# A fused attention and two-layer kernel: first output products inside the attention's plan, with new start and new places

## The chip, the cores and the metric

The kernel runs on one core of one Trainium2 chip. Times are device microseconds (us) from launch to end. An execution's profile gives its span, from the first to the last instruction, and the clock that TensorE was granted: 1.00 is its upper level of 2.4 GHz, 0.50 its lower of 1.2 GHz.

## The reference

```python
# q, k, v: (4, 8, 576, 64); tau a scalar
scores = scale * q @ k^T
thresh = max(scores) - tau
scores = where(scores >= thresh, scores, -1e9)
attn   = softmax(scores)              # sum + 1e-9
x      = attn @ v                     # as 2304 tokens x 512

# first layer, d_ff 1536
xn  = x / sqrt(mean(x * x) + 1e-6) * rms_g
g   = xn @ w_gate
x   = (silu(g) * (xn @ w_val)) @ w_out

# second layer, d_ff 2048
h   = x @ w2_in
out = (h * cos(h)) @ w2_out
```

The weights arrive in a wide number format; the kernel converts them on the chip. Products that need more than one pass are made from a high and a low half of each operand, three matmuls each (`mm3`).

## The kernel before

**Attention.** Heads are taken in 16 pairs, each cut into five units of up to 128 queries (`NU` = 80 units). For a pair, `load_k`, `load_q` and `load_v` issue its loads on SP's queue; `prep_pe` transposes keys ("b", "c") and queries ("a") on TensorE, and `prep_act` copies them out of PSUM on ScalarE. For a unit, `s_mm` makes scores in two PSUM tiles, `s_max` on VectorE moves them to SBUF with a running extreme, `s_exp` on ScalarE makes exponentials, `s_thr` on GpSimd the thresholds, and `s_mask` on VectorE the masked exponentials with their sums. `t_pe` and `c_pe` transpose these on TensorE, `t_raw` and `c_raw` copy them out, `av` multiplies by v into the one bank of the tag "v", and `av_out` copies the result. The sums are inverted (`r_inv`), written out (`r_out`) and read back over all partitions (`r_in`); `av_div` on GpSimd multiplies by them. Then `x_sq`, `x_add` (GpSimd) and `x_sum` (TensorE, into `pss`) make the mean square of each token, which is needed at the end of each batch of four pairs.

**The plan.** The order of the attention is not written by hand. `Plan.add` takes steps with an engine, a cost and a place from the table `STEPS`, and `Plan.order` simulates the engines. It repeatedly issues the step that can start first; `place`, which is the table's third number plus `at * UNIT`, decides between steps that can start at the same time. A TensorE step that changes the array's tiling (`TILING`: scores and `av`) can start only `SWITCH` (100 ns) later. Steps in `LOCK` keep VectorE and GpSimd apart in the simulation; those of `BEHIND` are also made to wait for the VectorE step ahead of them. `take` and `free` model the buffers: "t" has three PSUM banks, "v" one, "e" six. The engines then run their instructions in the issued order, each when its inputs are there.

At the start stand eight `warm` matmuls, two more behind the first transposes, and three after each of the first six units. While the attention runs, six weight jobs (`weight_job`, group 0 of the first layer) convert weights: a load, two integer steps on VectorE, one on ScalarE, one sum on GpSimd, then a high half on ScalarE and a low half by a subtraction on VectorE. The plan holds too the first chunk of the layer's input (`chunk(0, ...)`: `x_load`, `x_p`, `x_a`, `x_d`), chunks 1 and 2, and the first four gate and value products (`gv_mm` for n = 0 to 3, `N_EARLY`, each in two halves of 12 matmuls) with `h_silu`, `h_mul`, `h_hi` and `h_lo`.

**First layer.** Tokens go in six chunks of 384 and inner features in six groups of two tiles; `seq` lists (group, chunk, feature tile) as n = 0 to 71. Behind the plan a loop runs from n = 4: if `o1` is behind by more than one, an `o1` is run first; then come `gv_mm(n)` and `gv_h(n)`, and then the next `o1`. `o1(n)` multiplies with the output weights into four PSUM banks (`px`: three of "t" and the one of "v"); after the two tiles of a group it moves the four banks into `acc` on VectorE, by a copy in group 0 and by an addition later. `pump` advances the weight jobs between these steps. The second layer follows and is not touched.

Of the kernel before, what the change touches and what calls it, by code (L numbers as in the profile page):

```python
# [9 lines left out]
F32 = mybir.dt.float32  # L10
# [8 lines left out]
P = 128  # L19
# [6 lines left out]

UNIT = 3500
STEPS = {
    "none": ("", 0, 27559),
    "load_k": ("SP", 1700, -172962, 5000),  # L30
    "load_q": ("SP", 1700, -46102, 7000),
    "load_v": ("SP", 1700, -4761, 5000),
    "pb": ("PE", 440, -19143),
    "pa": ("PE", 440, -15661),
    "pc": ("PE", 330, -8379),
    "pb_a": ("ACT", 590, 81106),
    "pa_a": ("ACT", 690, -473960),
    "pc_a": ("ACT", 480, 49428),
    "s": ("PE", 960, -21325),
    "s4": ("PE", 490, 85459),  # L40
    "warm": ("PE", 640, 37404),
    "max": ("DVE", 833, -172383),
    "exp": ("ACT", 785, 72251),
    "th": ("POOL", 300, -18608),
    "mask": ("DVE", 890, -37373),
    "t": ("PE", 438, 31564),
    "raw": ("ACT", 595, -92045),
    "c0": ("PE", 220, -3639),
    "c1": ("PE", 440, -315186),
    "c_raw": ("ACT", 415, 218185),  # L50
    "radd": ("POOL", 250, 94231),
    "rinv": ("DVE", 430, -4519),
    "r_out": ("SP", 2100, -108544, 2500),
    "r_in": ("SP", 1700, -320774, 11000),
    "av0": ("PE", 2110, -371909),
    "av1": ("PE", 2660, -60188),
    "avo": ("ACT", 420, 4517),
    "div": ("POOL", 1410, 8372),
    "xout": ("SP", 500, -179658, 2500),
    "sq": ("POOL", 1145, 63241),  # L60
    "x_add": ("POOL", 1410, 86580),
    "xsum": ("PE", 1150, 399585),
    "mean": ("DVE", 150, -681609),
    "rms": ("POOL", 1520, 138440),
    "rs_out": ("SP", 2500, -32428, 2500),
    "x_load": ("SP", 500, 48239, 6000),
    "x_p": ("POOL", 1010, 169405),
    "x_a": ("ACT", 610, -116593),
    "x_d": ("DVE", 550, 94630),
    "jdma": ("SP", 500, 52341, 5000),  # L70
    "j1": ("DVE", 600, -115045),
    "j2": ("DVE", 690, -98093),
    "j_p": ("POOL", 1310, 466908),
    "j_a": ("ACT", 620, 67088),
    "gv": ("PE", 2100, 18969),
    "silu": ("ACT", 500, -124840),
    "hmul": ("DVE", 560, -259566),
    "hhi": ("ACT", 520, -319947),
    "hlo": ("DVE", 560, -244125),
}  # L80
SIGNAL = 100
SWITCH = 100

LOCK = {
    "mask", "j1", "j2", "x_d", "hlo", "th", "div", "sq", "x_add", "rms", "radd", "x_p", "j_p",
}
BEHIND = {"div", "sq", "x_add", "x_p", "j_p"}
# [9 lines left out]
N_EARLY = 4  # L97


class Plan:  # L100
# [19 lines left out]
    def order(self):  # L120
# [69 lines left out]
    def run(self, tc):  # L190


        done = tc.nc.cur_bb.bb.instructions
        wait = mybir.DependencyInfo(mybir.DependencyClass.Sync, mybir.DependencyReason.DATA)
        for s in self.order():
            n = len(done)
            s["fn"]()
            if s["eng"] == "DVE" and s["kind"] in LOCK:
                s["ins"] = done[-1]
            if s.get("behind"):  # L200
                for x in done[n:]:
                    tc.add_manual_dep(x, s["behind"]["ins"].name, wait, reason="port")


@with_exitstack
def attention_moe_cos_kernel(
# [81 lines left out]
    def weight_job(n, key, pool, stage, src, idle):  # L288
# [499 lines left out]
    def scale_x(c):  # L788
        nc.gpsimd.tensor_tensor(
            acc[c], acc[c], xrs[c][:, None, :].broadcast_to([P, KD, TC]), op=ALU.mult  # L790
        )

    def attention():

        plan = Plan({
# [23 lines left out]
        for p in range(NPAIRS):  # L819
            n = 5 * p  # L820
            if p:
                lk[p] = add("load_k", n, load_k, p, take=[("kn", ("kn", p))])
# [125 lines left out]
        for i, job in enumerate(jobs):  # L948
# [14 lines left out]
            jops.append(add("j2", at, step, after=[x], free=[("jtmp", i)] + ([] if wide else [("jraw", i)]),  # L963
            ))
        jobs.clear()

# [6 lines left out]
        def grow_2():  # L973
            att_s.close()
            late[2] = ctx.enter_context(tc.tile_pool(name="xhl2", bufs=1, side="right"))
            late["acc", 3] = ctx.enter_context(tc.tile_pool(name="acc3", bufs=1, side="right"))
            late["rs", 3] = ss_p

        ends = [mk[n, hd] for n in range(NU - 10, NU) for hd in heads(n)]
# [22 lines left out]
        for n in range(N_EARLY):  # L1002
# [6 lines left out]
            x = add("hmul", NU + n, h_mul, n, after=[x, y], free=[("gv", n)])  # L1009
            x = add("hhi", NU + n, h_hi, n, after=[x])  # L1010
            hs.append(add("hlo", NU + n, h_lo, n, after=[x], free=[("hh", n)]))
        plan.run(tc)

    with tc.manual_schedule():
        jobs += [
# [10 lines left out]
        acc_p = ctx.enter_context(tc.tile_pool(name="acc", bufs=NCH - 1))  # L1026
# [3 lines left out]
        late.update({("acc", c): acc_p for c in range(NCH) if c != 3})  # L1030
# [9 lines left out]
        xacc = {}  # L1040

        def o1(n):
            g, c, i = seq[n]
            fs = groups[g][1]
            if i == fs[0]:
                xacc[c] = [
                    (ps_t if d else ps_v).tile(
                        [P, 512], F32, tag="t" if d else "v", name=f"px{d}"
                    )[:, 0:TC]
                    for d in range(KD)  # L1050
                ]
            whi, wlo = slots["1", 2, i]
            h = hq.pop(n)
            for d in range(KD):
                mm3(xacc[c][d], (whi[:, d], wlo[:, d]), h, i == fs[0], i == fs[-1])
            if i == fs[-1]:
                if c not in acc:
                    acc[c] = acc_tile(c, [P, KD, TC])
                for d in range(KD):
                    dst = acc[c][:, d]  # L1060
                    if g == 0:
                        nc.vector.tensor_copy(dst, xacc[c][d])  # L1062
                    else:
                        nc.vector.tensor_tensor(dst, dst, xacc[c][d], op=ALU.add)
                del xacc[c]

        def split_x(c):
            for kk in range(KD):
# [191 lines left out]
```

## Time and profile before

| What | Value |
|---|---|
| Median of three runs | 1190.27 us (1190.05 to 1190.27) |
| Profiled execution, time | 1190.16 us |
| Its span | 1188.4 us |
| TensorE busy, of the span | 1162.2 us, 98% |
| VectorE busy | 798.9 us, 67% |
| ScalarE busy | 647.4 us, 54% |
| GpSimd busy | 313.8 us, 26% |
| Mean granted clock | 0.994 |

Engines are named PE (TensorE matmuls), PEld (its weight loads), DVE (VectorE), ACT (ScalarE), POOL (GpSimd) and SP (the queue that issues most loads). L524 is line 524 of the kernel. In a row "x<-y" reads as what is written and from what. A matmul's end is modelled, so consecutive rows can overlap a little; a matmul of two fp32 operands shows as two instructions. Idle time is given with the engine and line that ended it.

### The profile page before, as it was taken

The numbers are of one execution on the slowest core, as the hardware profiler recorded it, in microseconds if no ns is written. First come the engines' busy times: TensorE is split into PE (matmuls) and PEld (weight loads), VectorE is DVE, ScalarE is ACT, GpSimd is POOL, SyncE is SP. The second block draws the span as 40 slices with busy tenths as digits, with TensorE's granted clock in tenths as the row PEclk, the third lists the DMA queues.
The fourth block names the chain that finished last, engine by engine and source line by source line (L and its number), as shares of the span: only waits on it lengthen the run. The fifth ranks groups of instructions, "written<-read, shape, count | busy, mean of one in ns | idle before, by whom it ended". The sixth has DMA issues, their size and how long they took to land.

```text
span 1188.4 us, 18206 instructions
## 1 busy us (share of the span) xinstructions
PE 1162.2 (98%) x6832; PEld 1021.9 (86%) x6832; DVE 798.9 (67%) x1571; ACT 647.4 (54%) x1210; POOL 313.8 (26%) x299
## 2 busy tenths in 40 slices
PE   8999999999989999999999999999999999999997
PEld 6666666666779999999999999999999999999996
DVE  5787787877547572642735538579688696876765
ACT  5887877777424231321312214377676676766663
POOL 1223435423543120110201102014334243332222
PEclk9999999999989999999999999999999999999999
DMA  5434424112352130110300202102112021000014
GB/s 130 111 95 126 105 75 131 51 41 71 121 165 72 54 107 1 46 61 1 91 17 23 85 1 59 49 1 71 36 37 71 1 71 36 18 19 1 1 53 107
DMA packets 99448, 71.66 MB, mean 60 GB/s; under 512 B 65040, under 2 KB 89360, under 8 KB 99360
## 3 DMA queue, kind: packets, MB, share of 16 engines
q1 hardware_dynamic: 98256, 70.20, 21.0%
q8 instruction: 54, 0.88, 0.3%
q10 hardware_dynamic: 1040, 0.26, 0.1%
q14 instruction: 34, 0.28, 0.1%
q0 software_dynamic: 64, 0.03, 0.0%
HBM read 60.95 MB, written 9.52 MB: 59 GB/s over the span
## 4 chain that ended last, share of the span: by engine, by line
PE 91%; issue 3%; DVE 2%; ACT 1%; POOL 1%; DMA 1%; SPq 0%; POOLq 0%; DVEq 0%; ACTq 0%
PE pgv L736 23%; PE ph L736 16%; PE po L736 16%; PE px L736 11%; PE s L504 8%; PE po L630 7%; PE pst L593 5%; PE psc L612 1%; PE psa L438 1%; PE warm L702 0%; PE psb L438 0%; DMA raw<-in_moe_w_out_dram 0%; DVE wtmp L308 0%; DVE hlo L772 0%; ACT et L603 0%
## 5 line engine op out<-in xcount | busy, mean ns | idle before, releaser
L736 PE MATMUL pgv<-xl,whi 128*128 128x384 f32 x576 | 193.9, 337 | 0.0
L736 PE MATMUL pgv<-xh,whi 128*128 128x384 f32 x576 | 193.9, 337 | 0.0
L736 PE MATMUL pgv<-xh,wlo 128*128 128x384 f32 x576 | 193.7, 336 | 0.0
L312 POOL TENSOR_TENSOR wtmp<-wtmp,raw 128x512 int32<-128x512 int32 x68 | 93.5, 1375 | 364.4 <-DVE wtmp L308 347.7
L1165 POOL TENSOR_TENSOR hlo<-r,hhi 128x384 fp32r<-128x384 f32 x96 | 98.0, 1021 | 303.7 <-ACT hhi L1164 247.7
L760 ACT ACTIVATE hh<-pgv 128x384 f32<-128x384 f32 x72 | 35.4, 491 | 255.9 <-PE pgv L736 255.9
L764 DVE TENSOR_TENSOR hh<-hh,pgv 128x384 f32<-128x384 f32 x72 | 39.8, 552 | 167.0 <-ACT hh L760 166.9
L736 PE MATMUL ph<-xh,whi 128*128 128x384 f32 x384 | 129.7, 338 | 0.0
L736 PE MATMUL ph<-xl,whi 128*128 128x384 f32 x384 | 129.6, 338 | 0.0
L736 PE MATMUL ph<-xh,wlo 128*128 128x384 f32 x384 | 129.3, 337 | 0.0
L524 DVE TENSOR_SCALAR_CACHE_REDUCE s<-s 128x576 f32<-128x576 f32 x128 | 91.9, 754 | 47.3 <-PE s L504 47.1
L1147 ACT ACTIVATE t<-ph,magic 128x384 f32<-128x384 f32 x96 | 55.8, 581 | 111.4 <-PE ph L736 111.4
L736 PE MATMUL po<-whi,hlo 128*128 128x512 f32 x288 | 114.7, 398 | 1.4 <-POOL hlo L1165 1.4
L736 PE MATMUL po<-whi,hhi 128*128 128x512 f32 x288 | 113.9, 395 | 0.2 <-ACT hhi L1164 0.2
L736 PE MATMUL po<-wlo,hhi 128*128 128x512 f32 x288 | 113.5, 394 | 0.0
L736 PEld LDWEIGHTS pgv<-xl,whi 128*128 128x128 f32 x576 | 108.2, 188 | 0.4 <-DVE xl L730 0.3
L736 PEld LDWEIGHTS pgv<-xh,whi 128*128 128x128 f32 x576 | 108.3, 188 | 0.0
L736 PEld LDWEIGHTS pgv<-xh,wlo 128*128 128x128 f32 x576 | 108.2, 188 | 0.0
L553 DVE SCALAR_TENSOR_TENSOR e<-s,th,e 128x576 f32<-128x576 f32 x128 | 103.1, 840 | 0.5 <-POOL th L534 0.5
L736 PE MATMUL px<-hhi,whi 128*128 128x384 f32 x288 | 98.9, 343 | 3.6 <-DVE acc L1062 3.3
L1154 DVE SCALAR_TENSOR_TENSOR r<-t,r 128x384 f32<-128x384 f32 x96 | 99.4, 1035 | 3.3
L543 ACT ACTIVATE e<-s,m 128x576 f32<-128x576 f32 x128 | 95.7, 783 | 8.2 <-DVE s L524 7.9
(118 smaller groups left out, 2457.6 us busy)
## 6 DMA issues: line engine op xcount, KB each, us to landing
raw<-in_moe_w_out_dram SPq DMA_DIRECT2D x28, 512.0 KB
raw<-in_moe_w_in_dram SPq DMA_DIRECT2D x16, 512.0 KB
raw<-in_moe_w_gate_dram SPq DMA_DIRECT2D x12, 512.0 KB
raw<-in_moe_w_val_dram SPq DMA_DIRECT2D x12, 512.0 KB
x<-xb SPq DMA_DIRECT2D x16, 288.0 KB
kn<-in_k_dram SPq DMA_DIRECT2D x16, 256.0 KB
vn<-in_v_dram SPq DMA_DIRECT2D x16, 256.0 KB
qn<-in_q_dram SPq DMA_DIRECT2D x15, 256.0 KB
```

Source lines behind the costliest of these rows:

```text
L312: nc.gpsimd.tensor_tensor(tmp, tmp, lw, op=ALU.add)
L504: nc.tensor.matmul(ps[:, c, 0:288], lhs, kh[r, k0:k0 + 288], start=True, stop=True,)
L524: nc.vector.tensor_scalar(s.rearrange("p (c n) -> p c n", c=2), un[n].pop(("ps", hd))[:, :, 0:288], qscale[:, 0:1] if n % 5 == 4 else 1.0, ...
L543: nc.scalar.activation(un[n]["e"][:, hd], un[n]["s", hd], AF.Exp, bias=grp[group_of(n)]["m"][:, c], scale=-1.0)
L553: nc.vector.scalar_tensor_tensor(e, un[n].pop(("s", hd)), grp[group_of(n)]["th"][:, ci:ci + 1], e, op0=ALU.is_le, op1=ALU.mult, accum_out= ...
L593: nc.tensor.transpose(ps[:, c], e[:, hd, k0:k0 + P], ident)
L630: nc.tensor.matmul(po[64 * hd:64 * hd + 64, :], vn[:, c, hd, :] if c < 4 else vl[:, hd, :], hf[j]["et"][:, hd, c, :] if c < 4 else hf[j][" ...
L736: nc.tensor.matmul(ps, w[a], x[bb], start=first and i == 0, stop=last and i == 2)
L764: nc.vector.tensor_tensor(hq[n], hq[n], pgv.pop(n)[:, 1, 0:TC], op=ALU.mult)
L1147: nc.scalar.activation(t, ph, AF.Identity, bias=magic[:, 0:1], scale=INV2PI)
L1154: nc.vector.scalar_tensor_tensor(r, t, -C2, r, op0=ALU.mult, op1=ALU.add)
L1165: nc.gpsimd.tensor_tensor(lo, r, f(hi), op=ALU.subtract)
```

## The change

- The first chunk's output products `o1(0)` and `o1(1)` become steps of the attention's plan (`px`, `N_PX` = 2), with four copies `pxc`; the loop behind the plan begins at the third. Chunk 0's `acc` comes from a pool shared with chunk 3.
- In group 0 all chunks' copies of `px` to `acc` move from VectorE to ScalarE.
- Twelve warm-up matmuls stand at the start in place of eight, and none behind the first transposes in place of two. The second pair's key loads wait for the first key transposes.
- The low halves of group 0's weights are made on GpSimd (`j_l`) in place of VectorE, and the jobs' `at` grows by 8 a job in place of 2.
- Every place in `STEPS` is new, from hundred thousands down to millions; costs stay. The planner's test of buffers allows for one step that takes several buffers of one tag.

```diff
-    "s": ("PE", 960, -21325),
+    "s": ("PE", 960, -2737873),
-    "max": ("DVE", 833, -172383),
+    "max": ("DVE", 833, -2649268),
-    "exp": ("ACT", 785, 72251),
+    "exp": ("ACT", 785, 32433),
-    "mask": ("DVE", 890, -37373),
-    "t": ("PE", 438, 31564),
+    "mask": ("DVE", 890, -1204775),
+    "t": ("PE", 438, 1142305),
-    "rinv": ("DVE", 430, -4519),
+    "rinv": ("DVE", 430, 1875427),
-    "av1": ("PE", 2660, -60188),
+    "av1": ("PE", 2660, -1928172),
-    "x_p": ("POOL", 1010, 169405),
-    "x_a": ("ACT", 610, -116593),
-    "x_d": ("DVE", 550, 94630),
+    "x_p": ("POOL", 1010, 3517892),
+    "x_a": ("ACT", 610, 965899),
+    "x_d": ("DVE", 550, 477496),
+    "j_l": ("POOL", 1360, -80865),
-    "gv": ("PE", 2100, 18969),
+    "gv": ("PE", 2100, 618538),
+    "px": ("PE", 2100, -732741),
+    "pxc": ("ACT", 500, -135494),
...
-WARM = (8, 2, 0, 0)
+WARM = (12, 0, 0, 0)
...
-JOBS = 2
+JOBS = 8
+N_PX = 2
...
-                    held = [taken[tag][-self.bufs[tag]] for tag, _ in s["take"]
-                            if len(taken[tag]) >= self.bufs[tag]]
+                    tags = [tag for tag, _ in s["take"]]
+                    at = [(tag, len(taken[tag]) + tags[:i].count(tag) - self.bufs[tag]) for i, tag in enumerate(tags)]
+                    held = [taken[tag][i] for tag, i in at if i >= 0]
...
-        nc.vector.tensor_tensor(lo, w, f(hi), op=ALU.subtract)
+        (nc.vector if n else nc.gpsimd).tensor_tensor(lo, w, f(hi), op=ALU.subtract)
...
+    def px_mm(n):
+        g, c, i = seq[n]
+        fs = groups[g][1]
+        if i == fs[0]:
+            px_open(c)
+        whi, wlo = slots["1", 2, i]
+        h = hq.pop(n)
+        for d in range(KD):
+            mm3(xacc[c][d], (whi[:, d], wlo[:, d]), h, i == fs[0], i == fs[-1])
+
+    def px_out(g, c, d):
+        dst = acc[c][:, d]
+        if g == 0:
+            nc.scalar.copy(dst, xacc[c][d])
+        else:
+            nc.vector.tensor_tensor(dst, dst, xacc[c][d], op=ALU.add)
...
+            if kind == "b":
+                first = tc.nc.cur_bb.bb.instructions[-1]
...
+        def load_k1(p):
+
+            done_ = tc.nc.cur_bb.bb.instructions
+            n = len(done_)
+            load_k(p)
+            for x in done_[n:]:
+                tc.add_manual_dep(x, first.name, SYNC, reason="first loads")
...
+        y = add("none", 999, lambda: acc.__setitem__(0, acc_tile(0, [P, KD, TC])), after=[g2])
+        z = None
+        for n in range(N_PX):
+            z = add("px", NU + n + 3, px_mm, n, after=[hs[n], z],
+                take=[] if n else [("v", ("px", 0))] + [("t", ("px", d)) for d in range(1, KD)],
+            )
+        for d in range(KD):
+            add("pxc", NU + 5, px_out, 0, 0, d, after=[z, y], free=[("v" if not d else "t", ("px", d))] if 0 else [("px", d)])
...
-        done = 0
+        done = N_PX
```

## Rows read from the trace of the kernel before

**Rows 1.** Stretches: length, then busy us (instructions) by engine, clock, DMA share, GB/s
```profile
20.00:300.00 280.00, 273.38 (x2058) 182.96 (x2059) 224.06 (x613) 217.11 (x395) 96.05 (x110) 1.00 0.35 92
300.00:400.00 100.00, 91.49 (x527) 86.89 (x526) 58.37 (x97) 37.58 (x72) 44.99 (x32) 0.97 0.38 118
400.00:1150.00 750.00, 749.58 (x4016) 713.49 (x4015) 485.87 (x791) 367.10 (x700) 161.20 (x140) 1.00 0.12 37
```

**Rows 2.** Waits of TensorE: us in total, times, longest
```profile
PE s L504 <- DVE s L524: 5.2, 7, 0.9
PE pss L670 <- POOL sq L661: 4.9, 1, 4.9
PE px L736 <- DVE acc L1062: 3.3, 3, 1.7
```

**Rows 3.** The chain that ended last, 0 to 30 us: start, us, what
```profile
7.55 0.85 PE warm L702 x4
8.40 0.87 PE psa L438 x4
9.30 0.70 ACT q L470
...
10.04 1.57 PE s L504 x8
...
24.59 1.17 PE s L504 x8
25.76 0.58 PE psa L438 x4
```

**Rows 4.** One stretch of 1 us at the start, columns as in rows 1
```profile
8.00:9.00 1.00, 1.00 (x6) 1.00 (x6) 0.00 (x0) 0.17 (x1) 0.00 (x0) 0.50 0.00 0
```

**Rows 5.** Instructions in order of time at the start: start us, us, engine, line
```profile
1.03 3.41 PE L702 MATMUL warm<-ones 128*128 128x128 f32 x16 [1.03 <-DVE ones L354]
...
3.15 0.62 SPq L407 DMA_DIRECT2D kn<-in_k_dram  x1
...
6.87 0.30 PE L443 MATMUL psb<-ident,k 128*128 128x128 f32 x1 [2.44 <-DMA k<-in_k_dram]
...
7.59 0.58 ACT L472 COPY k<-psb 128x512 f32<-128x512 f32 x1 [4.83 <-PE psb L438]
```

**Rows 6.** The chain that ended last, 300 to 400 us
```profile
305.25 16.81 PE pgv L736 x96
...
359.48 2.12 PE px L736 x12
```

**Rows 7.** TensorE's instructions in order of time, with the idle time before them
```profile
144.50 1.17 PE L670 MATMUL pss<-ones,sq 128*128 128x1 f32 x10
...
329.79 2.29 PE L670 MATMUL pss<-ones,sq 128*128 128x1 f32 x10 [4.89 <-POOL sq L661]
...
335.52 0.34 PE L736 MATMUL pgv<-xh,whi 128*128 128x384 f32 x1
...
342.68 0.44 PE L736 MATMUL px<-hhi,whi 128*128 128x384 f32 x1 [0.75 <-DVE acc L1062]
...
353.00 0.41 PE L736 MATMUL px<-hhi,whi 128*128 128x384 f32 x1 [1.73 <-DVE acc L1062]
```

**Rows 8.** Single lines: ns min/median/max, first and last start
```profile
L553 DVE SCALAR_TENSOR_TENSOR e<-s,th,e x125: 775/814/1949, 21.4 to 298.6; 128x576 f32<-128x576 f32 x125
...
L1062 DVE COPY acc<-px x24: 541/547/552, 342.1 to 402.7; 128x384 f32<-128x384 f32 x24
...
L472 ACT COPY k<-psc x16: 460/472/485, 9.9 to 261.8; 128x384 f32<-128x384 f32 x16
```

**Rows 9.** Groups by line, 20 to 300 us: busy us, mean ns, idle before
```profile
L553 DVE SCALAR_TENSOR_TENSOR e<-s,th,e 128x576 f32<-128x576 f32 x125 | 100.7, 840 | 0.1
...
L322 DVE TENSOR_TENSOR wlo<-wtmp,whi 128x512 fp32r<-128x512 f32 x6 | 4.1, 688 | 0.0
...
L312 POOL TENSOR_TENSOR wtmp<-wtmp,raw 128x512 int32<-128x512 int32 x6 | 7.8, 1296 | 15.0 <-ACT e L543 6.1 <-DVE r L565 3.3 <-DVE e L553 2.6
```

More of the change, by code (lines that the diff above doesn't have):

```diff
@@ L28 @@
 STEPS = {
[L29 to L38, printed above, removed]
-    "s": ("PE", 960, -21325),
-    "s4": ("PE", 490, 85459),
-    "warm": ("PE", 640, 37404),
-    "max": ("DVE", 833, -172383),
-    "exp": ("ACT", 785, 72251),
@@ L59 @@
[L59 to L66, printed above, removed]
-    "x_p": ("POOL", 1010, 169405),
-    "x_a": ("ACT", 610, -116593),
-    "x_d": ("DVE", 550, 94630),
-    "jdma": ("SP", 500, 52341, 5000),
-    "j1": ("DVE", 600, -115045),
-    "j2": ("DVE", 690, -98093),
@@ L73 @@
-    "j_p": ("POOL", 1310, 466908),
-    "j_a": ("ACT", 620, 67088),
-    "gv": ("PE", 2100, 18969),
[L76 to L79, printed above, removed]
+    "none": ("", 0, 2360344),
+    "load_k": ("SP", 1700, -2424783, 5000),
+    "load_q": ("SP", 1700, -1835377, 7000),
+    "load_v": ("SP", 1700, 565279, 5000),
+    "pb": ("PE", 440, -924812),
+    "pa": ("PE", 440, -720087),
+    "pc": ("PE", 330, -813048),
@@ new lines @@
+    "pb_a": ("ACT", 590, -1433177),
+    "pa_a": ("ACT", 690, -1961837),
+    "pc_a": ("ACT", 480, -1532185),
+    "s": ("PE", 960, -2737873),
+    "s4": ("PE", 490, -247244),
+    "warm": ("PE", 640, -1788992),
+    "max": ("DVE", 833, -2649268),
+    "exp": ("ACT", 785, 32433),
+    "th": ("POOL", 300, 189602),
+    "mask": ("DVE", 890, -1204775),
+    "t": ("PE", 438, 1142305),
+    "raw": ("ACT", 595, -1387333),
+    "c0": ("PE", 220, -2636048),
+    "c1": ("PE", 440, 332505),
+    "c_raw": ("ACT", 415, -1227087),
@@ new lines @@
+    "radd": ("POOL", 250, -804037),
+    "rinv": ("DVE", 430, 1875427),
+    "r_out": ("SP", 2100, -946810, 2500),
+    "r_in": ("SP", 1700, 229333, 11000),
+    "av0": ("PE", 2110, -3347974),
+    "av1": ("PE", 2660, -1928172),
+    "avo": ("ACT", 420, -921309),
+    "div": ("POOL", 1410, -1170463),
+    "xout": ("SP", 500, -495711, 2500),
+    "sq": ("POOL", 1145, 2068614),
+    "x_add": ("POOL", 1410, 1803440),
+    "xsum": ("PE", 1150, -533107),
+    "mean": ("DVE", 150, -2130499),
+    "rms": ("POOL", 1520, -174766),
@@ new lines @@
+    "rs_out": ("SP", 2500, 3402942, 2500),
+    "x_load": ("SP", 500, 1165958, 6000),
+    "x_p": ("POOL", 1010, 3517892),
+    "x_a": ("ACT", 610, 965899),
+    "x_d": ("DVE", 550, 477496),
+    "jdma": ("SP", 500, -91861, 5000),
+    "j1": ("DVE", 600, -2635108),
+    "j2": ("DVE", 690, -1758570),
+    "j_l": ("POOL", 1360, -80865),
+    "j_p": ("POOL", 1310, 3397281),
+    "j_a": ("ACT", 620, 29748),
+    "gv": ("PE", 2100, 618538),
+    "silu": ("ACT", 500, 72147),
+    "px": ("PE", 2100, -732741),
@@ L80 @@
+    "pxc": ("ACT", 500, -135494),
+    "hmul": ("DVE", 560, 36994),
+    "hhi": ("ACT", 520, 1636981),
+    "hlo": ("DVE", 560, -2086549),
 }
@@ L84 @@
 LOCK = {
-    "mask", "j1", "j2", "x_d", "hlo", "th", "div", "sq", "x_add", "rms", "radd", "x_p", "j_p",
+    "mask", "j1", "j2", "x_d", "hlo", "th", "div", "sq", "x_add", "rms", "radd", "x_p", "j_p", "j_l",
 }
-BEHIND = {"div", "sq", "x_add", "x_p", "j_p"}
+BEHIND = {"div", "sq", "x_add", "x_p", "j_p", "j_l"}
 TILING = {"s": 1, "s4": 3, "av0": 2, "av1": 2}
-WARM = (8, 2, 0, 0)
+WARM = (12, 0, 0, 0)
 WARM_S = (3, 3, 3, 3, 3, 3)
@@ L95 @@
 X0 = 45
-JOBS = 2
+JOBS = 8
 N_EARLY = 4
+N_PX = 2
+SYNC = mybir.DependencyInfo(mybir.DependencyClass.Sync, mybir.DependencyReason.DATA)
 class Plan:
@@ L193, in run @@
         done = tc.nc.cur_bb.bb.instructions
-        wait = mybir.DependencyInfo(mybir.DependencyClass.Sync, mybir.DependencyReason.DATA)
         for s in self.order():
@@ L201, in run @@
                 for x in done[n:]:
-                    tc.add_manual_dep(x, s["behind"]["ins"].name, wait, reason="port")
+                    tc.add_manual_dep(x, s["behind"]["ins"].name, SYNC, reason="port")
 @with_exitstack
@@ L791, in scale_x, with px_open, o1 @@
         )
+    xacc = {}
+    def px_open(c):
+        xacc[c] = [
+            (ps_t if d else ps_v).tile([P, 512], F32, tag="t" if d else "v", name=f"px{d}")[:, 0:TC]
+            for d in range(KD)
+        ]
+    def px_mm(n):
[13 more added lines that the diff above has]
+            nc.vector.tensor_tensor(dst, dst, xacc[c][d], op=ALU.add)
+    def o1(n):
+        g, c, i = seq[n]
+        px_mm(n)
+        if i == groups[g][1][-1]:
+            if c not in acc:
+                acc[c] = acc_tile(c, [P, KD, TC])
+            for d in range(KD):
+                px_out(g, c, d)
+            del xacc[c]
     def attention():
@@ L821, in attention @@
             if p:
-                lk[p] = add("load_k", n, load_k, p, take=[("kn", ("kn", p))])
+                lk[p] = add("load_k", n, load_k if p > 1 else load_k1, p, take=[("kn", ("kn", p))])
                 lq[p] = add("load_q", n, load_q, p, take=[("qn", ("qn", p)), ("q4", ("q4", p))]
@@ L962, in attention @@
             x = add("j_a", at, step, gen, 2, after=[x])
-            jops.append(add("j2", at, step, after=[x], free=[("jtmp", i)] + ([] if wide else [("jraw", i)]),
+            jops.append(add("j_l", at, step, after=[x], free=[("jtmp", i)] + ([] if wide else [("jraw", i)]),
             ))
@@ L975, in grow_2 @@
             late[2] = ctx.enter_context(tc.tile_pool(name="xhl2", bufs=1, side="right"))
-            late["acc", 3] = ctx.enter_context(tc.tile_pool(name="acc3", bufs=1, side="right"))
+            late["acc", 3] = late["acc", 0] = ctx.enter_context(
+                tc.tile_pool(name="acc3", bufs=2, side="right")
+            )
             late["rs", 3] = ss_p
@@ L1011, in attention @@
             hs.append(add("hlo", NU + n, h_lo, n, after=[x], free=[("hh", n)]))
+        y = add("none", 999, lambda: acc.__setitem__(0, acc_tile(0, [P, KD, TC])), after=[g2])
[3 more added lines that the diff above has]
+                take=[] if n else [("v", ("px", 0))] + [("t", ("px", d)) for d in range(1, KD)],
+            )
+        for d in range(KD):
+            add("pxc", NU + 5, px_out, 0, 0, d, after=[z, y], free=[("v" if not d else "t", ("px", d))] if 0 else [("px", d)])
         plan.run(tc)
+        xacc.pop(0)
     with tc.manual_schedule():
@@ L1025, in attention_moe_cos_kernel @@
         x_p = ctx.enter_context(tc.tile_pool(name="xhl", bufs=NCH - 3))
-        acc_p = ctx.enter_context(tc.tile_pool(name="acc", bufs=NCH - 1))
+        acc_p = ctx.enter_context(tc.tile_pool(name="acc", bufs=NCH - 2))
         m2 = ExitStack()
@@ L1029, in attention_moe_cos_kernel @@
         late.update({c: x_p for c in range(3, NCH)})
-        late.update({("acc", c): acc_p for c in range(NCH) if c != 3})
+        late.update({("acc", c): acc_p for c in range(NCH) if c not in (0, 3)})
         late.update({("rs", c): t_rs for c in range(4, NCH)})
@@ L1037, in attention_moe_cos_kernel @@
                     jobs.append((n, (str(lay), kd, i), w_b if pool else w_a, stage, src, IDLE1 if len(jobs) < 3 else 1))
[L1040 to L1065, printed above, removed]
         def split_x(c):
```

11 lines of the change are left out of this document (removed).

## The prediction

> **What bounds the kernel now.** I began with the busy time by stage. From 400 to 1150 us TensorE is busy for 749.58 of 750 us, so nothing the change does there can pay [rows 1]. Between 20 and 300 us, the attention, TensorE is busy for 273.38 of 280 us: 6.6 us are idle. Between 300 and 400 us, the passage into the first layer, 8.5 us are idle. So I look for gains at the start, in the passage, and only a little in the attention.
>
> The table of TensorE's waits says who ends the idle time: the first products `px` wait 3.3 us for VectorE's copies out of PSUM, `pss` waits 4.9 us once for GpSimd, and the scores `s` wait 5.2 us for VectorE's `s_max` [rows 2].
>
> At the start I followed the chain that ended last. TensorE waits for the first keys until 6.87 [rows 5]; behind their transposes come two warm-up matmuls (0.85 us), the four transposes of q (0.87), ScalarE's scaled copy (0.70) and the first scores (1.57) [rows 3]. The same scores and transposes take 1.17 and 0.58 us later in that chain [rows 3]: the granted clock at 8 to 9 us was 0.50, the 1.2 GHz level, after TensorE had stood idle for 2.4 us before the keys [rows 4, 5].
>
> In the passage the chain shows 96 gate and value matmuls in 16.81 us [rows 6], then the last `av`. After that comes the wait for GpSimd's division, square and sum. What follows runs slowly: `pss` takes 2.29 us against 1.17 us at 144.50, and the first `px` step, from the end of `pss` (329.79 + 2.29 = 332.08) until `pgv` starts at 335.52, takes 3.4 us against 2.12 us later [rows 6, 7].
>
> **The parts and their costs.** The sum is made against the profiled execution, 1190.16 us (span 1188.4 us), 0.11 us below the median of 1190.27.
>
> *Start.* The twelve early warm-up matmuls are 24 instructions; at 3.41 us for 16 [rows 5] they last 5.1 us and end at about 6.15, before the keys come. The idle time before the first transposes shrinks from 2.4 to 0.7 us, so I expect the clock not to fall at 8 us. Removing the two later ones takes 0.85 us off TensorE's line, and the transposes shrink by 0.87 - 0.58 = 0.29. ScalarE's copy of q then begins behind its copy of the first keys (7.59 to 8.17 [rows 5]) and the scores start at about 8.9 instead of 10.04: -1.1 us. The scores themselves shrink by 1.57 - 1.17 = 0.4. The second keys' loads, issued at 3.15 [rows 5], now wait for the first transposes, and no longer share the DMA engines with the first keys and queries. That may bring the keys forward by nothing, or by 0.7 at most, where the warm-up ends; I take 0.4. Together -1.9 us, bounds 0 and -2.2. Zero is possible because SP stands behind that wait: every load that it issues for the next pairs is queued there, and TensorE would wait for those instead.
>
> *Output products in the plan.* `o1(0)` and `o1(1)` move from after the attention's plan into it; after it `done` begins at 2. No matmul is saved. What is certain is the catching up: before, the loop ran two `o1` in a row at n = 4, 5 and 6, so a chunk's products followed directly upon the last ones in the same PSUM banks and waited for four copies: 0.75 us at 342.68 and 1.73 us at 353.00 [rows 7]. Now a `gv_mm` stands between them (a quarter of 16.81, so 4.2 us of TensorE), which hides the copies, and chunk 0's are made inside the plan. That is -2.5 us, bounds -1 and -3.3 (all three of such waits [rows 2]).
>
> *Copies on ScalarE.* 24 copies of 547 ns leave VectorE; ScalarE's nearest, a 128x384 copy out of PSUM, takes 472 ns [rows 8]. Four are 1.9 us on either engine and lie beside a `gv_mm`. Should that cover go, each chunk costs up to 1.9 us. In the sum: 0.
>
> *Does the early work fill the wait of 4.9 us?* This decides the size. The plan always takes the step that can start first, and `place` breaks ties only; a step of `av` starts `SWITCH` later than one that needs no change of tiling. So while a `gv` or `px` can start, the planner does not start the last `av`. Worse, `px` takes the single "v" bank, and the last `av` waits for it until the copies are done. I expect the order gv, px, gv, av, and then the same chain of division, square and sum with nothing beside it. The `px` go before the wait rather than into it: 0 us. If the last `av` goes first, the gain is 4.9 + (2.29 - 1.17) + (3.4 - 2.1) = 7.3 us.
>
> *Low halves on GpSimd, spread, and all new places.* Six VectorE instructions of 688 ns (4.1 us) become six on GpSimd at about 1296 ns, by the nearest form, in this stage [rows 9]. VectorE is not the bound, but it ends TensorE's 5.2 us of waits. The places reorder every engine's queue; the trace of before cannot show the result. Best is all 6.6 us of idle gone. Worst, I take the longest of the score waits, 0.9 us [rows 2], at each of 15 joints between pairs, in place of the present 5.2: 13.5 - 5.2 = +8.3 us. I take -1.0, near nothing, a quarter of the 4.1 us.
>
> GpSimd can hold VectorE up: the longest mask took 1949 ns against a median of 814 [rows 8]. But over 125 masks the mean is 840 ns [rows 9], 26 ns above the median, 3.3 us in all beside 96 us of GpSimd work [rows 1]. By that ratio six operations of 1.3 us cost 0.3 us.
>
> The Trainium skill (SBUF — State Buffer, Who interferes with whom) speaks against this edit: a VectorE operation with both inputs in SBUF and a GpSimd operation that reads SBUF exclude each other, and whoever comes second is blocked for the whole instruction. By it each of the six could hold back a mask for its full length, and the sum would end near the fifth case below instead of at its own figure. The longest mask agrees; the mean shows that it is rare here, where the plan starts such steps behind a VectorE operation.
>
> Sum: -1.9 - 2.5 + 0 + 0 - 1.0 = -5.4 us: 1190.16 - 5.4 = 1184.8 us.
>
> **The rivals.**
> 1. *As summed, the wait for `pss` stays*: 1184.8 us; alone 1180 to 1188. For it: the tie rule and the one "v" bank.
> 2. *The wait is filled*: 1184.8 - 7.3 = 1177.5 us. It needs the last `av` ahead of some 5 us of gv or px, so chunk 0's last `x_d` must come about 1 us after the last transposes. Its steps x_p, x_a and x_d stand far back in the new places, which speaks for it; in the trace of before the gates followed the transposes without a gap, which speaks against.
> 3. *Nothing measurable*: the start's 1.9 us and the copies' 2.5 us are got, but the new order takes 4.4 us back, or the loads behind SP's wait take the first: 1190 us.
> 4. *Slower: the attention's order makes TensorE wait.* With places so far apart, transposes are always last on TensorE and scores nearly first; the transposes free the six `e` buffers, without which ScalarE's exponentials stand, and the masks behind them. Price: 0.9 us at each pair's joint, +8.3 us, so 1190.16 - 4.4 + 8.3 = 1194.1 us. It decides from 6.8 us of added wait on. Against it: TensorE has been idle for just 6.6 us in that stage.
> 5. *GpSimd blocks VectorE*: six blocks of 1.3 us are 7.8, less the 4.1 removed, +3.7 us in place of -1.0: 1189.5 us. It is the page's rule at its full price.
>
> **How the numbers follow.** About 0.2% (2.4 us) is what a measurement of this kernel can tell from no change. Chances: first 0.42, second 0.27, third 0.12, fourth 0.14, fifth 0.05. The second and nearly all of the first are faster (0.68), with some of the third at the better end: faster 0.71. Same: the third and fifth, 0.15. Slower: 0.14. The likeliest gives 1184.8 us. For the range I leave out the better half of the second (below 1176) and most of the fourth (above 1190.5): 1176 to 1190.5 us.
>
> **What would show it.** Start: granted clock 1.00 between 8 and 10 us, first scores near 8.2 to 8.9. Catching up: no wait of `px` for a copy in the first chunks, the copies under ScalarE. The decisive row is TensorE's wait at `pss`: about 4.9 us under the first case, none under the second, with the order of the last `av` and the first `px` beside it. Attention: TensorE's idle time between 20 and 300 us, 6.6 us now. The prediction is wrong if `pss` no longer waits, if that idle time grows by more than 5 us, or if TensorE waits for the second pair's keys or queries at the start.

## The result, and the profile after

The changed kernel takes 1178.8 us (median of four executions, 1178.0 to 1179.61) against 1190.27: the ratio is 0.9901 [0.9884, 0.9918], 11.5 us less. The forecast was 1184.8 us. The profiled execution took 1179.61 us with a span of 1177.4, 11.0 us less than the 1188.4 before.

The span can be cut at two events that both traces show: TensorE's first scores, and the end of the attention's last transposes. What lies between the second and the start of the last `pgv` matmul is called the passage here.

| | before | after | difference | forecast |
|---|---|---|---|---|
| first scores start | 10.04 | 8.52 | -1.5 | -1.5 |
| from there to the last transposes' end | 295.21 | 293.44 | -1.8 | -1.4 |
| passage, to the last `pgv` | 465.83 | 458.14 | -7.7 | -2.5 |

Of the start's forecast of -1.9 us, 0.4 is the shortening of the first scores themselves; it falls behind their start, so it stands in the second row. So 5.2 of the 5.6 us by which the profiled span was missed lie in the passage. Its stretches, with the columns of [rows 1]:

```profile
8.00:10.00 2.00, 1.50 (x11) 0.99 (x11) 0.21 (x1) 0.84 (x2) 0.00 (x0) 1.00 0.56 129
20.00:300.00 280.00, 278.17 (x2073) 186.74 (x2072) 220.67 (x607) 218.66 (x397) 103.52 (x119) 1.00 0.35 91
300.00:400.00 100.00, 97.55 (x560) 94.95 (x559) 53.27 (x75) 47.47 (x97) 42.60 (x29) 0.98 0.37 118
400.00:1150.00 750.00, 749.57 (x4010) 712.46 (x4009) 489.88 (x795) 371.70 (x708) 165.00 (x143) 1.00 0.13 38
...
358.00:362.00 4.00, 4.00 (x16) 3.94 (x15) 3.39 (x8) 2.23 (x4) 0.00 (x0) 0.57 0.00 0
```

TensorE's idle time fell from 8.5 to 2.45 us between 300 and 400 us and from 6.6 to 1.8 us in the attention [rows 1]. The first row is the start: the granted clock is now 1.00 there, where [rows 4] had 0.50. The waits of TensorE, to be read beside [rows 2]:

```profile
PE pgv L743 <- DVE xl L737: 1.8, 1, 1.8
...
PE po L637 <- ACT et L610: 1.1, 3, 0.7
...
PE s L511 <- DVE s L531: 0.9, 1, 0.9
```

The waits at `pss` (4.9) and of `px` for copies (3.3) are gone, the seven score waits have become one, and a new wait of `pgv` for `xl` has come. The chain through the passage says how, in the columns of [rows 6]:

```profile
302.08 0.52 ACT et L610
302.60 0.04 issue
302.64 2.91 PE po L637 x20
305.55 8.54 PE pgv L743 x48
314.09 2.12 PE px L743 x12
316.21 2.12 PE pgv L743 x12
318.33 2.12 PE px L743 x12
320.45 4.24 PE pgv L743 x24
324.69 1.01 PE pss L677 x10
325.70 2.19 PE pgv L743 x12
327.90 2.08 PE px L743 x12
```

`po` is the last `av`. It goes first, and both `px` steps stand behind it and ahead of `pss`. `pss` takes 1.01 us in this chain and the next `px` step 2.08, where they took 2.29 and 3.4 behind the wait [rows 7].

### The profile page after: what moved, and what is told of

The parts are those of the page before. It is cut to its first block, busy times and chain, and to the rows that moved or that the text cites. A ratio compares the mean times of both kernels' runs of the same rounds, so it can differ in the third digit from the quotient of the medians.

```text
span 1177.4 us, 18232 instructions
## 1 busy us (share of the span) xinstructions
PE 1164.0 (99%) x6836; PEld 1024.7 (87%) x6836; DVE 788.0 (67%) x1541; ACT 657.5 (56%) x1234; POOL 319.8 (27%) x305
## 4 chain that ended last, share of the span: by engine, by line
PE 93%; issue 3%; ACT 2%; DVE 1%; POOL 0%; POOLq 0%; ACTq 0%
PE pgv L743 24%; PE ph L743 16%; PE po L743 16%; PE px L743 12%; PE s L511 8%; PE po L637 7%; PE pst L600 5%; PE warm L709 1%; PE psc L619 1%; ACT et L610 1%; PE psa L445 1%; PE psb L445 0%; PE pss L677 0%; DVE wtmp L315 0%; DVE wtmp L310 0%
## 5 line engine op out<-in xcount | busy, mean ns | idle before, releaser
L1202 POOL TENSOR_TENSOR hlo<-r,hhi 128x384 fp32r<-128x384 f32 x96 | 98.2, 1023 | 303.8 <-ACT hhi L1201 248.1
L560 DVE SCALAR_TENSOR_TENSOR e<-s,th,e 128x576 f32<-128x576 f32 x128 | 100.7, 820 | 0.9 <-POOL th L541 0.7
L743 PE MATMUL px<-hlo,whi 128*128 128x384 f32 x288 | 97.8, 340 | 0.1
```

The source lines that it names most:

```text
L560: nc.vector.scalar_tensor_tensor(e, un[n].pop(("s", hd)), grp[group_of(n)]["th"][:, ci:ci + 1], e, op0=ALU.is_le, op1=ALU.mult, accum_out= ...
L743: nc.tensor.matmul(ps, w[a], x[bb], start=first and i == 0, stop=last and i == 2)
L1202: nc.gpsimd.tensor_tensor(lo, r, f(hi), op=ALU.subtract)
```

## The experiments

All ratios are to the kernel before on the same chip, with a 95% interval. "Idle" and "clock" are TensorE's between 300 and 400 us; the passage is measured as above. These three come from the traced execution, which isn't always near the median: it took 1188.52 us for b_av_px and 1187.47 us for a_av_last.

| kernel | us | ratio | idle | clock | passage |
|---|---|---|---|---|---|
| before | 1190.27 | | 8.5 | 0.97 | 465.8 |
| b_av_first | 1190.74 | 0.9999 [0.9990, 1.0008] | 9.1 | 0.98 | 466.1 |
| b_px | 1191.3 | 1.0001 [0.9993, 1.0010] | 8.6 | 0.93 | 467.2 |
| b_av_px | 1186.04 | 0.9957 [0.9944, 0.9971] | 5.2 | 0.95 | 464.3 |
| b_px_in_wait | 1181.88 | 0.9922 [0.9909, 0.9936] | 3.1 | 1.00 | 457.7 |
| after | 1178.8 | 0.9901 [0.9884, 0.9918] | 2.45 | 0.98 | 458.1 |
| a_no_px | 1185.03 | 0.9951 [0.9939, 0.9963] | 7.0 | 0.97 | 464.1 |
| a_av_last | 1185.62 | 0.9961 [0.9949, 0.9974] | 7.0 | 0.95 | 466.5 |
| a_px_in_wait | 1180.17 | 0.9906 [0.9892, 0.9919] | 2.7 | 0.98 | 458.7 |
| a_scale4 | 1176.61 | 0.9882 [0.9868, 0.9895] | 1.3 | 1.00 | 455.7 |
| a_scale_dve | 1176.52 | 0.9881 [0.9868, 0.9895] | 1.55 | 1.00 | 455.7 |

The last three columns belong together. As an estimate, a base of 453.7 us (fitted to the changed kernel), plus the idle time, plus 1 us for each 0.01 of clock lost in those 100 us, gives each passage within 1.4 us (b_px: 2.1, where much of the low clock falls into idle time). For the change that is 6.1 us of idle time and about 1 us of clock, out of 7.7.

### The order of the last av and the first px

**b_av_first**: before, with the last `av` ahead of the gates.

```diff
-            x = add("gv", NU + n, gv_mm, n, 0, after=(x0, x1)[c] + jops + [smm[NU - 1], g1],
+            x = add("gv", NU + n, gv_mm, n, 0, after=(x0, x1)[c] + jops + [smm[NU - 1], g1, last_av],
```

> The kernel before, with one edit: the first gate step waits in the plan for the last av, so that this goes first; places, px and start as before. Theory (the order of the last av made the largest term): the wait of 4.9 us before pss goes, and with it the slow pss (1.1) and the slow first px (1.3), less a short wait of about 0.7 of the last av for its copies; 1190.3 - 6.6 = 1183.7 us, no wait of TensorE at pss. Rival (the early px are what fills the wait, the order alone does not): 1188 us or more, and the wait at pss stays above 3 us.

```profile
306.79 0.71 PE L630 MATMUL po<-ec,v 128*64 128x320 f32 x4
...
327.72 1.28 PE L670 MATMUL pss<-ones,sq 128*128 128x1 f32 x10 [3.19 <-POOL sq L661]
...
336.09 0.44 PE L736 MATMUL pgv<-xl,whi 128*128 128x384 f32 x1 [1.60 <-DVE xl L730]
```

In these rows of TensorE's timeline the last `av` is done at 307.5, with 17 us of `pgv` behind it, and `pss` still waits 3.19 us. GpSimd's timeline tells why: the division of the pair before the last starts at 314.81, after 4.26 us of waiting for a step of VectorE, its square waits 2.22 us in the same way, and the last pair's division comes behind them at 323.55. So GpSimd's queue sets `pss`, not the `av`, and TensorE has run out of other work. A new wait for `xl` takes 1.6 us more. The order of `av` alone is worth nothing, as the rival said.

**b_px**: the kernel before with the output products as steps of the plan, the copies on ScalarE, and everything else old (places, start, low halves). The new steps `px` and `pxc` have no old place and get those of `gv` and `silu`.

```diff
+N_PX = 2
...
+            z = add("px", NU + n + 3, px_mm, n, after=[hs[n], z],
...
-        done = 0
+        done = N_PX
```

> The kernel before with px of the first chunk in the plan and group 0's copies on ScalarE; places, start, low halves and spread as before, and the last av still behind the gates. Theory now (in the passage TensorE waits for GpSimd's queue; it needs both the last av early and the px as work beside it, neither alone): only the catching up is saved, 1187.5 to 1190 us, with a wait of 4 to 5 us at pss. Rival (each of the two alone has its own gain of about 6 us): 1184 us.

The chain from the end of the gates:

```profile
321.87 0.71 PE pgv L742 x4
322.57 4.25 PE px L742 x24
...
326.85 0.48 ACT acc L821
327.32 0.50 ACT xh L732
327.83 3.40 POOL acc L795
331.22 1.08 issue
332.30 1.41 POOL xb L653
...
333.78 1.16 POOL sq L663
...
335.00 1.41 POOL sq L667
...
336.45 2.29 PE pss L676 x10
338.74 4.04 PE px L742 x12
...
369.87 5.83 PE pgv L742 x23
```

This is the forecast's order, gv, px, gv, av, and the forecast's result: nothing gained. It shows more than was forecast. With the `av` as late as 326.74, the 3.40 us scaling of chunk 3 (`acc`) stands ahead of the division (`xb`) in GpSimd's order, and the wait at `pss` grows to 6.80 us. The rows behind the waits are slow: the granted clock is 0.50 from 334 to 342 us.

**b_av_px**: b_px with the last `av` ahead of the gates, by the edit of b_av_first.

> As the one before this, and the first gate step waits in the plan for the last av: both together, with before's places and start. Theory (the two only pay together): no wait at pss, 1190.6 - 6 to 8 = 1182.6 to 1184.6 us. Rival (the new places are needed beyond the order of the last av): 1187 us or more.

No wait at `pss`; three waits for `xl` (1.76, 1.01, 1.78) stay, with a clock of 0.95. Together the two edits are worth 4.5 us, each alone nothing. The five executions lie between 1184.25 and 1188.52 us, and their median falls between what the theory and the rival had.

**b_px_in_wait**: b_px with the last `av` behind all gates, and `px` behind that `av`.

```diff
+            if n == N_EARLY - 1:
+                last_av["after"].append(last_gv)
...
-            z = add("px", NU + n + 3, px_mm, n, after=[hs[n], z],
+            z = add("px", NU + n + 3, px_mm, n, after=[hs[n], z, last_av],
```

> The kernel before with the output products in the plan and their copies on ScalarE (the kernel of the run with these alone, which took 1191.3 us and waited 6.8 us at pss), and those products behind the last av instead of ahead of it; the last av stays behind all gate and value matmuls. Theory: the place of px decides, not that of av: GpSimd's chain starts 4.2 us earlier and px lies beside it, the wait shrinks to about 2.6 us and the time is 1186 to 1187 us, as with the early av. Rival: GpSimd's queue before that chain (the scaling, the pairs before) sets pss, the wait stays and the time is 1191 us within 0.6.

TensorE's, then GpSimd's instructions in order of time:

```profile
321.97 2.37 PE L636 MATMUL po<-et,vn 128*64 128x320 f32 x16
...
325.41 0.45 PE L742 MATMUL px<-hhi,whi 128*128 128x384 f32 x1 [0.52 <-ACT t L646]
...
329.85 1.28 PE L676 MATMUL pss<-ones,sq 128*128 128x1 f32 x10
...
325.43 1.43 POOL L653 TENSOR_TENSOR xb<-t,rb 128x576 f32<-128x576 f32 x1 [1.83 <-ACT t L646]
...
331.67 3.80 POOL L795 TENSOR_TENSOR acc<-acc,rs 128x1536 f32<-128x1536 f32 x1
```

`pss` starts at 329.85, as in the kernel before (329.79 in [rows 7]), but the 24 `px` matmuls, which stood behind it there, are done. The scaling now follows the chain. Against b_px, with the same work, it is 9.4 us faster, more than the theory's 4 to 5. Two things differ: the `av`, no longer behind `px`, starts 4.8 us earlier (0.5 of it from the attention), and the scaling is out of the division's way. TensorE idles 5.5 us less between 300 and 400 us, and what ran slowly in b_px (`pss` 2.29, `px` 4.04, 23 `pgv` 5.83) takes 1.28, 2.08 and 4.32 us here, 4.5 us less; together that is 0.5 us more than the passage's 9.5. So the early `av` isn't needed; what pays is that `px` lies between the last `av` and `pss`.

**a_no_px**, **a_av_last** and **a_px_in_wait** ask the same from the other side: the changed kernel without `px` in the plan (`N_PX` = 0), with the last `av` behind the last gate, and with that and `px` behind the `av` (the two edits shown for b_px_in_wait).

> The changed kernel with N_PX = 0: no px in the plan, the loop behind it starts with o1(0) as before; copies on ScalarE, places and start stay. Theory: only the catching up comes back, waits of px for the copies of 1 to 3 us in all; 1180 to 1182 us, still no wait at pss. Rival (px in the plan made the largest term): 1184 us or more.

> The changed kernel with one edit: the last av waits in the plan for the last gate step, so the early px stay in the plan but lie ahead of it. Theory: the wait of about 4.9 us at pss comes back, with the slow pss and the slow work after it; 1178.8 + 6 to 7.5 = 1185 to 1186 us. Rival (the early px are what fills the wait): at most 1180.5 us.

> The changed kernel with the last av behind the last gate and value matmuls, and chunk 0's output products behind that av, so that they stand inside the wait for GpSimd. Theory: what counts is the TensorE work that lies beside GpSimd's chain; two px steps of 2.1 us fill 4.2 of the 4.7 us that pss waited with the last av late, and about 1181 to 1182 us come out. Rival: px is not what is short, the chain must begin early, since GpSimd's queue is longer than all that is left; then TensorE waits at pss or behind it just as long and the time is 1184.5 us or more.

Without `px`, `pss` waits 1.48 us and `pgv` 4.3 us for `xl`: 6.2 us lost. With the `av` late and `px` ahead of it, `pss` waits 4.70 us: 6.8 lost. With `px` moved behind that late `av`, `pss` waits 0.3 and 1.4 us are lost. The early `av` itself is thus worth 1.4 us at most; the intervals of the two kernels overlap. These rows are TensorE's and GpSimd's in a_av_last, then TensorE's in a_px_in_wait:

```profile
331.55 2.12 PE L677 MATMUL pss<-ones,sq 128*128 128x1 f32 x10 [4.70 <-POOL sq L668]
...
319.65 3.51 POOL L796 TENSOR_TENSOR acc<-acc,rs 128x1536 f32<-128x1536 f32 x1
327.40 1.40 POOL L654 TENSOR_TENSOR xb<-t,rb 128x576 f32<-128x576 f32 x1 [4.24 <-ACT t L647]
...
327.29 1.28 PE L677 MATMUL pss<-ones,sq 128*128 128x1 f32 x10 [0.31 <-POOL sq L668]
```

In a_av_last the scaling is done at 323.16, and GpSimd then stands until the copy of the `av` comes. So the order of `av` and `px` alone, without the scaling in the way, moves `pss` by 4.26 us here, and the kernel's time by 5.4.

### The new wait for xl

The timeline of the changed kernel, of TensorE, VectorE and GpSimd in turn:

```profile
357.07 0.45 PE L743 MATMUL pgv<-xl,whi 128*128 128x384 f32 x1 [1.77 <-DVE xl L737]
...
352.50 3.98 DVE L329 TENSOR_TENSOR wlo<-wtmp,whi 128x512 fp32r<-128x512 f32 x1
356.41 2.19 DVE L737 SCALAR_TENSOR_TENSOR xl<-acc,g_sb,xh 128x384 fp32r<-128x384 f32 x4
358.53 0.68 DVE L329 TENSOR_TENSOR wlo<-wtmp,whi 128x512 fp32r<-128x512 f32 x1
...
352.12 3.81 POOL L796 TENSOR_TENSOR acc<-acc,rs 128x1536 f32<-128x1536 f32 x1
```

TensorE waits for `xl`, which stands on VectorE behind a low half of a weight. That low half takes 3.98 us, against 0.68 for the same form 2 us later, and it ends 0.55 us after GpSimd's scaling of chunk 5, beside which it ran. Behind the wait the granted clock is 0.57, mostly the lower level, from 358 to 362 us (last row of the first fence), and the next 23 `pgv` take 5.84 us in the chain where 24 usually take 4.16.

**a_scale4** cuts the scaling into four operations, **a_scale_dve** gives it whole to VectorE (`nc.vector` in place of `nc.gpsimd`).

```diff
     def scale_x(c):
-        nc.gpsimd.tensor_tensor(
-            acc[c], acc[c], xrs[c][:, None, :].broadcast_to([P, KD, TC]), op=ALU.mult
-        )
+        for kk in range(KD):
+            nc.gpsimd.tensor_tensor(acc[c][:, kk], acc[c][:, kk], xrs[c], op=ALU.mult)
```

> The changed kernel with scale_x cut into four GpSimd operations of 128x384 in place of one of 128x1536. Theory (at 352 us VectorE's low half took 3.98 us because GpSimd's long operation of 3.81 us held it; that delayed the chunk's low part, on which TensorE waited 1.8 us and then ran at the lower clock): held operations shrink to below 2.2 us, the wait of 1.8 us goes; 1175.5 to 1177.5 us. Rival (VectorE has too much of its own work there): 1178 to 1179.6 us, the wait stays.

> The changed kernel with scale_x on VectorE in place of GpSimd. Theory (GpSimd holds VectorE): VectorE does the same in about 1.6 us and is no longer held; 1175.5 to 1177.5 us. Rival (VectorE has too much of its own work): 1180 us or more.

With four operations, these are TensorE's wait for `xl`, the group on GpSimd from 300 to 400 us, and the low half on VectorE:

```profile
PE pgv L743 <- DVE xl L737: 0.5, 1, 0.5
...
L797 POOL TENSOR_TENSOR acc<-acc,rs 128x384 f32<-128x384 f32 x12 | 14.5, 1236 | 1.8 <-DVE hlo L779 1.8
...
350.03 1.79 DVE L329 TENSOR_TENSOR wlo<-wtmp,whi 128x512 fp32r<-128x512 f32 x1
```

GpSimd needs more time for a chunk (4 x 1.24 = 4.9 us instead of 3.8 to 4.0), but this low half is held for 1.1 us instead of 3.3, the clock stays at 1.00, and 2.2 us are won. VectorE isn't free of GpSimd with that: the four `xl` behind the low half now take 4.73 us in place of 2.19, but they start at 352.52 in place of 356.41. On VectorE the scaling takes 1.76 us at the median and wins as much. That the long GpSimd operations made the wait is shown by both. Not shown is which of them: earlier in the chain to this wait a conversion on VectorE took 3.73 us beside the scaling of chunk 4 (last section), and both edits change all three scalings. The Trainium skill (SBUF — State Buffer, Who interferes with whom) has the shared ports of the two engines as an exclusive lock that blocks the second comer for the whole instruction; the trace agrees: 3.98 us of a 0.68 us form, beside 3.81.

### The copies, the low halves, their spreading, the places and the start

| kernel | edit | us | ratio |
|---|---|---|---|
| a_copy_dve | after, group 0's copies on VectorE | 1178.25 | 0.9893 [0.9880, 0.9907] |
| a_best | a_scale_dve and a_copy_dve together | 1177.49 | 0.9888 [0.9875, 0.9902] |
| a_low_same | after, low halves on VectorE, all orders kept | 1178.09 | 0.9896 [0.9883, 0.9910] |
| a_low_dve | after, low halves on VectorE as `j2` steps of the plan | 1203.13 | 1.0097 [1.0081, 1.0112] |
| a_jobs2 | after, `JOBS` = 2 | 1184.63 | 0.9936 [0.9923, 0.9950] |
| b_places | before, `STEPS` of after | 1192.84 | 1.0016 [1.0008, 1.0025] |
| b_start | before, `WARM = (12, 0, 0, 0)` and the held key loads | 1189.12 | 0.9983 [0.9974, 0.9992] |

```diff
# a_copy_dve
-            nc.scalar.copy(dst, xacc[c][d])
+            nc.vector.tensor_copy(dst, xacc[c][d])
# a_low_same; a_low_dve has this and the next
-        (nc.vector if n else nc.gpsimd).tensor_tensor(lo, w, f(hi), op=ALU.subtract)
+        nc.vector.tensor_tensor(lo, w, f(hi), op=ALU.subtract)
# a_low_dve
-            jops.append(add("j_l", at, step, after=[x], free=[("jtmp", i)] + ([] if wide else [("jraw", i)]),
+            jops.append(add("j2", at, step, after=[x], free=[("jtmp", i)] + ([] if wide else [("jraw", i)]),
```

> The changed kernel with the copies of the first group's output products on VectorE again instead of ScalarE. Theory, as in the prediction: a chunk of gate and value matmuls hides the four copies on either engine, so the time stays at 1178.8 us within 1. Rival: VectorE has the splitting of the scaled x in the same stretch and is held by GpSimd there, so the wait of gv for the low half grows and px waits for copies again; then 1180 us or more.

> The changed kernel with the scaling of chunks 1 to 3 on VectorE instead of GpSimd and the first group's copies back on VectorE. If the copies are hidden on either engine, 1176.5 us as with the scaling alone; if VectorE becomes short in the passage with both, 1177.5 us or more.

The copies' engine makes no difference that can be told in the changed kernel. With the scaling (of chunks 3 to 5, not 1 to 3) on VectorE, `px` waits 0.8 us for VectorE's copy again, and about 1 us of a_scale_dve's time is lost.

> The changed kernel with every step where the plan puts it, and the low halves of the first group's weights computed by VectorE instead of GpSimd; the order of TensorE's instructions is the same. Theory: the attention's 1.8 us came with these operations' leaving VectorE; it takes 295 us again and the time is 1180 to 1181 us. Rival: it came from the order of the new places and the spreading; 1178.8 us within 0.6.

> The changed kernel with the low halves of the first group's weights back on VectorE (still spread out, same places). Theory: the attention's 1.8 us came from these six operations leaving VectorE, which ends TensorE's waits for the scores; then the attention takes about 295 us again and the time is 1180 to 1181 us. Rival: the gain there came from the new places and the spreading of the weights' steps; then 1178.8 us within 0.6.

With the order kept, six subtractions of 1278 ns on GpSimd or of VectorE's 0.69 us give the same time, and TensorE's idle time in the attention is the same 1.8 us. The theory that the attention's gain came from VectorE's relief fell, in the main: the attention is 294.07 us long, against 293.44 to 293.49 in the other eight kernels with this order, so 0.6 of the 1.8 us may belong to it. a_low_dve was no test of it: the other kind of step has another engine, cost and place in the table and isn't in `BEHIND`, the plan let the first `pgv` start at 300.28, ahead of the last transposes (334.81), and those `pgv` then stood waiting for `xh` with the transposes queued behind them:

```profile
320.17 0.69 PE L743 MATMUL pgv<-xh,whi 128*128 128x384 f32 x1 [5.82 <-ACT xh L733]
...
334.81 1.47 PE L600 MATMUL pst<-ident,e 128*128 128x128 f32 x12
```

Planning six small steps as another kind costs 24 us; which of its four differences does it isn't shown.

> The changed kernel with the weights' steps at two places of each other as before, instead of eight, so that they come early in the attention and not spread over it. Theory: the spreading is a part of the attention's 1.8 us; 1179.5 to 1181 us, with more waits of TensorE for VectorE's maxima in the first 100 us. Rival: the plan's new order elsewhere decides and the time is 1178.8 us within 0.6; or the places do not fit these steps any more, and it loses several us.

> The kernel before with the new table of places and nothing else. Theory: the new places alone put the last av ahead of the gates (-6.6 us) and order the attention a little better (-1.8 us): about 1182 us, no wait at pss. Rival (the places do little, px in the plan and the start made the change): 1188 to 1191 us.

The spreading is worth 4 to 6 us (4.2 by the ratios, 5.8 by the medians; its executions lie between 1181.8 and 1184.91), but not where the theory had it: the attention is as long without it (293.48 us). What it lost is in the passage, where TensorE waits 5.0 us for `xl` in three waits. The places alone do harm: the last `av` goes first with them, `pss` waits 5.50 us, and the attention is 295.94 us long.

> The kernel before with twelve early warm-up matmuls, none later, and the second pair's key loads held behind the first transposes, nothing else. Theory: the start is worth 1.5 us by itself, first scores near 8.5 us instead of 10.04, and 1188.5 to 1189.3 us. Rival: what is won at the start is lost in the attention, where the scores wait for VectorE anyway; then 1190.3 us within 0.5.

The start brings 0.9983 [0.9974, 0.9992], some 2.0 us, by itself; the first scores start at 8.52, as in the changed kernel, with a clock of 1.00. The stretch behind that is 294.91 us long, 0.3 less than before.

## Why the prediction was wrong

**The step that failed** is "Does the early work fill the wait of 4.9 us?", and in it: "I expect the order gv, px, gv, av ... The `px` go before the wait rather than into it: 0 us." The second rival, with a chance of 0.27, is what happened: av, gv, px, gv, px, gv, `pss`. The step's reasoning from order to time holds, since b_px has the expected order and gains nothing. The rule of the planner that it rests on stands too: a step which can start first wins, and the places break ties only. What failed is the premise, drawn from the trace of before, that a gate can start as soon as the transposes end. A gate needs the last `xl` of chunk 0 (the step `x_d`); VectorE's rows, before and after:

```profile
303.18 0.61 DVE L730 SCALAR_TENSOR_TENSOR xl<-x,g_sb,xh 128x384 fp32r<-128x384 f32 x1
...
303.13 0.62 DVE L737 SCALAR_TENSOR_TENSOR xl<-x,g_sb,xh 128x384 fp32r<-128x384 f32 x1 [3.57 <-ACT xh L733]
```

It is done at 303.8 in both. But the last transposes end at 305.25 before, 1.5 us behind it, and at 301.96 after, 1.8 us ahead of it. So no gate can start there: TensorE stands 0.68 us until ScalarE's copies let the last `av` start, at 302.64. With the places of after alone (b_places) that is so already: the transposes end at 306.28, `xl` at 307.08, and the `av` starts at 307.29. These are the chip's times; the planner's own are in no row.

**The rival's condition was not the right one either.** It asked for the last `av` ahead of some 5 us of gv or px. b_av_first has 17 us of gv behind the `av` and gains nothing, because the gates are used up before GpSimd's queue is done; b_px_in_wait has the `av` as late as before and gains 8.4 us by the medians, 9.3 by the ratio. TensorE's work behind the last `av` has to last until GpSimd's sum is there: behind an early `av` the gates and `px` together do it (b_av_px), and behind a late one `px` alone (b_px_in_wait). The rival's price, 7.3 us on top of the forecast's other terms, gave 1177.5 us, 1.3 below the result; the new wait for `xl` (1.77 us) and the low clock behind it (5.84 - 4.16 = 1.7) took back 3.5 us which no case of mine held. That the number comes so close is thus partly luck: with these 3.5 us counted, the same sum would have fallen 1.8 us short of the profiled span's gain of 11.0.

**Catching up (-2.5).** The waits of `px` for copies are gone, all 3.3 us of them. But b_px, where they are gone too, gains nothing: the longer wait at `pss` and one for `xl` of 1.8 us took it. The term can't be summed apart from the wait at `pss`. Nor was the catching up itself the cause: in a_no_px the loop runs two `o1` in a row as before, and `px` waits only 0.6 us for copies, but `pgv` 4.3 us for `xl`.

**Copies on ScalarE (0)** was right, by a_copy_dve.

**The start (-1.9)** was right: the warm-up lasts 5.49 us (5.1 forecast), the keys' transposes start at 6.59 (6.87 before), and the clock stays up:

```profile
1.03 5.49 PE L709 MATMUL warm<-ones 128*128 128x128 f32 x24 [1.03 <-DVE ones L361]
6.59 0.33 PE L450 MATMUL psb<-ident,k 128*128 128x128 f32 x1
...
8.52 0.76 PE L511 MATMUL s<-k,q 64*128 64x288 f32 x4 [0.50 <-ACT q L477]
...
8.52 1.24 PE s L511 x8
```

The scores start at 8.52, the forecast's 8.9 less the 0.4 for earlier keys, and in the chain (last row) they take 1.24 us in place of 1.57 [rows 3]: 1.85 us in all. No load waits behind SP's queue showed up.

**The attention (-1.0)** came out at -1.8, of which 0.3 is the shorter first scores, the start's term; 1.5 remain. The share put down to the low halves is 0.6 us at most (a_low_same). Neither the spreading (a_jobs2) nor `px` in the plan (a_no_px) nor the start (b_start) gives or takes the rest, and the places alone make the attention longer (b_places). What is left is the new places together with low halves planned as GpSimd steps; no run has just these two, so the source stays open. GpSimd's low halves did not block masks at a price that can be seen: the fifth case was wrong about its place. Its mechanism came in the passage instead, by the scaling that was already there.

**What stays open**: the rest of the attention's gain; which of the two held VectorE operations made the wait for `xl`; and why the clock fell behind some waits and not others (below).

## What to carry to other kernels

When an engine waits at the end of a chain, list the work that could stand inside the wait, and put it behind the step that starts the chain and ahead of the wait; the same 24 matmuls, moved from ahead of a late last `av` to behind it, were worth 9.4 us in one kernel and 5.4 us in the other. Where a greedy planner makes the order, a forecast about one wait is a forecast about that order: work it out step by step, or hold both orders as cases of equal weight, since six small steps planned as another kind moved 24 us. When a wait is filled, look at what is late next: here cutting each GpSimd scaling of 3.8 us into four gave 2.2 us more: 1176.5 to 1176.71 us, below every execution of both kernels.

## What the runs showed of the hardware that I had not expected

- The idle share is not the time. In the attention TensorE's idle time fell by 4.8 us, its length by 1.8, with the same number of matmul instructions but one (2164 and 2163): from the first scores to the last transposes it was busy for 288.59 us before and for 291.61 after. A part of what shows as waiting before shows as longer matmuls after, whose ends are modelled; which, the runs don't tell.
- A wait of TensorE of nearly the same length is followed by a lower clock or isn't. After 1.77 us at 357.07 the changed kernel ran at 0.57 for 4 us; in b_px_in_wait a wait of 1.67 us at 361.37 left the clock at 1.00. The changed kernel's four executions lie at 1178.00, 1178.03, 1179.56 and 1179.61 us; the step of 1.5 us between them is about what that stretch cost in the profiled one (1179.61). That the two shorter ones did not have it isn't shown: their mean clocks over the span are 1.000 and 0.998, those of the longer ones 0.998 and 0.997.
- A VectorE operation with one input is held too: the conversion at L310 took 3.73 us at 345.27, beside the scaling of chunk 4 (3.96 us from 344.75), where its median is 0.418.
